# Third tiles paired for a Strassen-Winograd out projection, and attention pieces moved between halves

## The chip, the cores and the metric

The kernel runs on one core of a Trainium2 chip. The metric is the device time in microseconds: the median of several executions. A core has five engines that run side by side, each with its own instruction stream in order: TensorE (PE; matmuls from SBUF into PSUM; PEld in the profile is its load of stationary operands), VectorE (DVE), ScalarE (ACT), GpSimd (POOL) and SyncE (SP, which here only issues transfers). They wait for each other through semaphores. PSUM has eight banks of 512 float32 columns per partition.

## What is computed

A local attention, and on its output a feed-forward block with a relu gate (cut to what matters):

```
# attention: q, k, v of shape (4 batches, 8 heads, 768 positions, 64)
scores = q @ k.T / 8 - slope[head] * distance     # kept: 96 positions back, and 8 global keys
a = softmax(scores);  x = a @ v                    # x: (3072 tokens, 512)
# feed-forward, d_model 512, d_ff 1536
h = relu(x @ w_gate) * (x @ w_val)
out = h @ w_out                                    # (3072, 512)
```

## The kernel before

The 3072 tokens are taken as eight halves (half a batch, 384 tokens each), numbered c = 0 to 7; `s` numbers the same halves in the attention. A half has three tiles of 128 tokens, n = 0, 1, 2.

*The feed-forward block of a half* is built by `ffn_pieces(c)` (L509) as two lists of items with a weight each, f1 and f2. f1 has, for each of the twelve blocks `fc` of 128 hidden columns, a gate (four matmuls of 384 columns with `wg`, then a relu on ScalarE, L525) and a val (four matmuls with `wv`, then a product with the relu on VectorE into `ht`, L531). From half 2 on the first two items are split (`begin`): six of the eight matmuls of fc = 0 first, then the last quarter of the gate and of the val, which need the last part of `xT`.

f2 is the out projection. In half 0 it is plain: for each tile, four items of three matmuls of 512 columns (`outp`, L538), a copy on ScalarE, a store. From half 1 on only the third tile is plain; tiles 0 and 1 are taken together by Strassen's scheme: the four blocks are two tiles by two halves of the hidden columns, and seven products (p1 to p7) of six matmuls with 256 columns each (`block`, L583) replace eight. They use sums of activations (`sum_cb`, `sum_ad`, `sum_de` on VectorE, L567, L571, L576), five sums of weight blocks, computed once in half 1 (`wo_sum`, L809), three ScalarE copies from PSUM and six VectorE passes (L611 to L629) that combine the products into two float32 tiles `osb`. Two products (p6, p7) add onto a bank that holds p3 or p1 already. Some sums are put behind val items (`behind`), the others between the items of f2.

*The attention of a half* is a list of 26 pieces from `attention_pieces(s)` (L493), in four pairs of heads p. `piece_qk(s, p, g)`: g = 0 issues all scores of the pair into four PSUM banks (`pair_scores`, L397) and two exps (L406); g = 1 the other two exps and the masks of the first two banks on VectorE (L359); g = 2 the other masks. `piece_av(s, p, e)`: five (or four) matmuls with the values (L427), a log on ScalarE (L436) and, for e = 1, an exp (L441) that gives the reciprocal of the sums. `piece_norm(s, p)`: two VectorE products (L446) that write `xT`. An empty piece, `gap`, keeps some apart.

*The early pieces* of a half s bring queries and keys: casts on GpSimd (L363), three transposing transfers on SyncE (L368), and GpSimd copies that put the keys in order (L259 to L265). Loads of q and k are issued on SyncE and those of v on GpSimd, at the start of a half's turn.

*The order* is written out by hand. In turn c, `weave` (L664) issues the items of f1 + f2 of half c and, after each, every placed piece whose position (a fraction of the summed weights) has been reached. `spread` (L659) gives evenly spaced positions: in turn c the attention of half c + 1 stands between 0.0 and 0.8 (0.07 and 0.82 for c = 2), the early pieces of half c + 2 between 0.25 and 0.75. Half 0's last third, half 1's last third and their out projections are woven with the attention of half 2, whose last piece, the norm of the last pair, is issued after everything else of that turn. Half 7 has no attention beside it. Each engine takes its instructions in the order in which they were issued.

PSUM from half 1's last third on: three banks "ff" for gates, vals and some products, five banks "x" for attention and the other products, each pool used in rotation. `ht` has two buffers, `osb` three.

Of the kernel before, what the change touches and what calls it, by code (L numbers as in the profile page):

```python
# [8 lines left out]
FP32 = mybir.dt.float32  # L9
BF16 = mybir.dt.bfloat16  # L10
AF = mybir.ActivationFunctionType
ALU = mybir.AluOpType
# [3 lines left out]
def kernel(  # L16
# [12 lines left out]
    nc = tc.nc  # L29
# [4 lines left out]
    DM = H * D  # L34
# [473 lines left out]

    def ffn_pieces(c):  # L509
# [43 lines left out]

        N2, D2 = N_FC // 2, DM // 2
        tiles_ = [slice(n * 128, (n + 1) * 128) for n in range(2)]

        def sums_of(name, *shape):
            if name not in st:
                st[name] = late["sums"].tile([128, *shape], BF16, name=name)
            return st[name]  # L560

        cb = lambda: sums_of("cb", N2, 2, 128)
        ad = lambda: sums_of("ad", N2, 128)
        de = lambda: sums_of("de", N_FC, 128)

        def sum_cb(i0, i1):
            nc.vector.tensor_tensor(cb()[:, i0:i1].rearrange("f i n t -> f i (n t)"), ht[:, i0:i1, 0:256],  # L567
                                    ht[:, N2 + i0 : N2 + i1, 0:256], op=ALU.add)

        def sum_ad(i0, i1):  # L570
            nc.vector.tensor_tensor(ad()[:, i0:i1], ht[:, i0:i1, tiles_[0]],  # L571
                                    ht[:, N2 + i0 : N2 + i1, tiles_[1]], op=ALU.add)

        def sum_de(i0, i1):
            x, y = (1, 0) if i0 < N2 else (0, 1)
            nc.vector.tensor_tensor(de()[:, i0:i1], ht[:, i0:i1, tiles_[x]], ht[:, i0:i1, tiles_[y]],  # L576
                                    op=ALU.subtract)

        def block(key, pool, left, right, start, stop):
            if start:  # L580
                st[key] = psum[pool].tile([128, 512], FP32, name=f"{pool}_ps")
            for i in range(N2):
                nc.tensor.matmul(st[key][:, 0:D2], lhsT=left(i), rhs=right(i),  # L583
                                 start=start and i == 0, stop=stop and i == N2 - 1,
                                 skip_group_check=not start)
            return st[key][:, 0:D2]

        c0, c1 = slice(0, D2), slice(D2, DM)
        bs = lambda name: lambda i: late["bs"][name][:, i]
        V2 = nc.vector.tensor_tensor  # L590

        def store(n, cols, eng=nc.sync):
            eng.dma_start(out=out_v[c, n][:, cols], in_=st["r", n][:, cols])

        def p4():
            for n in range(2):
                st["r", n] = late["osb"].tile([128, DM], FP32, name="osb")
            ps = block("d", "ff", lambda i: ht[:, N2 + i, tiles_[1]], bs("b21-b11"), True, True)
            nc.scalar.copy(st["r", 0][:, c0], ps)

        def p3():
            ps = block("c", "ff", lambda i: ht[:, i, tiles_[0]], bs("b12-b22"), True, True)
            nc.scalar.copy(st["r", 0][:, c1], ps)

        def p1():
            ps = block("a", "ff", lambda i: ad()[:, i], bs("b11+b22"), True, True)
            nc.scalar.copy(st["r", 1][:, c1], ps)

        def p2():
            ps = block("b", "x", lambda i: cb()[:, i, 1], lambda i: wo_sb[:, i, c0], True, True)  # L610
            V2(st["r", 1][:, c0], ps, st["r", 0][:, c0], op=ALU.add)  # L611
            V2(st["r", 1][:, c1], st["r", 1][:, c1], ps, op=ALU.subtract)

        def p5():
            ps = block("e", "x", lambda i: cb()[:, i, 0], lambda i: wo_sb[:, N2 + i, c1], True, True)
            V2(st["r", 0][:, c1], ps, st["r", 0][:, c1], op=ALU.add)
            V2(st["r", 0][:, c0], st["r", 0][:, c0], ps, op=ALU.subtract)
            if c == NHALF - 1:
                store(1, c0)
                store(0, c1)  # L620

        def p6():
            ps = block("c", "ff", lambda i: de()[:, i], bs("b11+b12"), False, True)
            V2(st["r", 1][:, c1], ps, st["r", 1][:, c1], op=ALU.add)
            store(1, slice(0, DM) if c < NHALF - 1 else c1, nc.sync if c < NHALF - 1 else nc.scalar)

        def p7():
            ps = block("a", "ff", lambda i: de()[:, N2 + i], bs("b21+b22"), False, True)
            V2(st["r", 0][:, c0], ps, st["r", 0][:, c0], op=ALU.add)  # L629
            store(0, slice(0, DM) if c < NHALF - 1 else c0)  # L630

        behind = {2: [lambda: sum_de(0, 3)], 5: [lambda: sum_de(3, 6)], 8: [lambda: sum_cb(0, 3)],
                  9: [lambda: sum_ad(0, 3)], 10: [lambda: sum_de(6, 9)]}

        def val_and_sums(fc):
            val(fc)
            for f in behind.get(fc, ()):
                f()

# [7 lines left out]
        if c >= 2:  # L647
            f1[:2] = [(1.0, begin_of[c][0]), (0.15, begin_of[c][1]), (0.15, begin_of[c][2])]
# [230 lines left out]
```

## Time and profile before

| | us |
|---|---|
| median of 3 executions | 241.33 (241.17 to 242.48) |
| the profiled execution | 241.74 |
| its span, first to last instruction | 239.9 |
| mean granted TensorE clock | 0.998 of full speed |

| turn | from, us | what TensorE does |
|---|---|---|
| start, halves 0 and 1 | 0 to 79 | attention 0 and 1, feed-forward 0 and 1, attention 2 |
| half 2 | 79 to 104.8 | feed-forward 2, attention 3 |
| half 3 | 104.8 to 131.4 | feed-forward 3, attention 4 |
| half 4 | 131.4 to 159.2 | feed-forward 4, attention 5 |
| half 5 | 159.2 to 186.2 | feed-forward 5, attention 6 |
| half 6 | 186.2 to 213.8 | feed-forward 6, attention 7 |
| half 7 | 213.8 to 236.6 | feed-forward 7 |

The page gives each engine's busy time, the chain of work that ended last, and groups of instructions by source line. "L583 PE MATMUL ... x84 | 10.3, 272 | 0.0" reads: line 583, 84 matmuls, busy 10.3 us in all, 272 ns for one, no idle time in front of them. Matmuls overlap, so one lasts longer than the distance between two starts; the distance is read from the timeline, whose rows give start, length, engine, line, operation, tiles, shape and count, and in brackets the engine's idle time before and what ended it.

### The profile page before, as it was taken

To read this page: it belongs to the slowest core of one execution; us is meant where nothing else is said; L and a number is where in the kernel's file an instruction comes from. 1 tells how busy PE (TensorE), PEld (TensorE's weight loads), DVE (VectorE), ACT (ScalarE), POOL (GpSimd) and SP (SyncE) were. 2 spreads that over 40 slices of the span, in tenths; PEclk is the share of its full clock that TensorE was granted. 3 is DMA by queue.
4 is the path that set the end of the run, shared out by engine and by line. 5 is a ranking of instruction groups with operands and counts; after the bars stand their busy time and mean duration, and the time that the engine had idled before them with its cause. 6 is when DMAs were issued, how large, how long until landed. Compare 5 with 4: busy or idle time off the path is not lost.

```text
span 239.9 us, 5355 instructions
## 1 busy us (share of the span) xinstructions
PE 233.5 (97%) x1937; PEld 146.6 (61%) x1945; DVE 173.3 (72%) x456; ACT 153.4 (64%) x347; POOL 85.9 (36%) x202
## 2 busy tenths in 40 slices
PE   7899999999999999999999999999999999999994
PEld 3655555665458566666668566676658566676663
DVE  7775955869677788777787687866887677764643
ACT  5897883337775777748774777638774677733330
POOL 6767893208414860903274060902350000000000
PEclk9999999999999999999999999999999999999999
DMA  6999999993976997098519939398431200030003
GB/s 200 181 198 177 257 234 219 185 162 61 270 178 134 301 150 131 8 185 257 108 25 122 285 93 133 19 166 262 67 68 44 90 0 0 3 129 3 4 27 104
DMA packets 69603, 31.42 MB, mean 131 GB/s; under 512 B 47160, under 2 KB 66616, under 8 KB 69576
## 3 DMA queue, kind: packets, MB, share of 16 engines
q0 software_dynamic: 31744, 8.71, 35.3%
q1 hardware_dynamic: 36616, 21.45, 35.1%
q10 hardware_dynamic: 1216, 0.92, 1.2%
q8 instruction: 15, 0.25, 0.4%
q14 instruction: 12, 0.10, 0.1%
HBM read 28.41 MB, written 6.29 MB: 145 GB/s over the span
## 4 chain that ended last, share of the span: by engine, by line
PE 91%; ACT 3%; DVE 2%; issue 1%; ACTq 0%
PE ff_ps L518 53%; PE ff_ps L538 9%; PE ff_ps L583 8%; PE x_ps L427 6%; PE x_ps L397 4%; PE x_ps L583 3%; PE t_ps L459 2%; PE s_ps L341 2%; PE t_ps L272 1%; PE t_ps L682 1%; ACT lnd L436 1%; PE t_ps L310 1%; DVE xT L446 1%; PE s_ps L321 1%; ACT rcp L441 0%
## 5 line engine op out<-in xcount | busy, mean ns | idle before, releaser
L518 PE MATMUL ff_ps<-xT,wg 128*128 128x384 bf16 x384 | 80.7, 326 | 0.5 <-ACT grelu L525 0.4
L518 PE MATMUL ff_ps<-xT,wv 128*128 128x384 bf16 x384 | 80.2, 326 | 0.0
L531 DVE TENSOR_TENSOR ht<-ff_ps,grelu 128x384 bf16<-128x384 f32 x96 | 53.1, 554 | 28.5 <-PE ff_ps L518 13.8
L525 ACT ACTIVATE grelu<-ff_ps 128x384 bf16<-128x384 f32 x96 | 47.1, 492 | 39.4 <-PE ff_ps L518 20.9
L518 PEld LDWEIGHTS <-wg 128*128 128x128 bf16 x384 | 35.9, 98 | 23.9 <-issue 0.9
L518 PEld LDWEIGHTS <-wv 128*128 128x128 bf16 x384 | 36.1, 97 | 23.4 <-issue 1.2
L406 ACT ACTIVATE es<-x_ps 128x360 bf16<-128x360 f32 (+2 forms) x96 | 36.8, 444 | 16.9 <-PE x_ps L397 16.8
L359 DVE TENSOR_TENSOR es<-es,m_all 128x432 bf16<-128x432 bf16 (+4 forms) x108 | 31.2, 334 | 8.2 <-ACT es L406 7.8
L446 DVE TENSOR_TENSOR xT<-x_ps,rcp 64x384 bf16<-64x384 f32 x48 | 26.6, 554 | 9.4 <-ACT rcp L441 8.8
L436 ACT ACTIVATE lnd<-x_ps 64x384 f32<-64x384 f32 x48 | 23.3, 485 | 12.5 <-PE x_ps L427 11.8
L538 PE MATMUL ff_ps<-wo_sb,ht 128*128 128x512 bf16 x112 | 29.6, 379 | 0.4
L363 POOL CAST kqc<-ks 128x384 bf16<-128x384 f32 x24 | 11.6, 532 | 32.3 <-DMA ks<-in_k_dram 32.3
L137 POOL DMA_DIRECT2D vbuf<-in_v_dram x25 | 21.6, 880 | 2.6 <-DMA wv<-in_moe_w_val_dram 2.1
L427 PE MATMUL x_ps<-es,vbuf 128*128 128x216 bf16 (+4 forms) x216 | 21.8, 225 | 0.0
L427 PEld LDWEIGHTS <-vbuf 128*128 128x128 bf16 x216 | 15.8, 97 | 7.7
L538 PEld LDWEIGHTS <-ht 128*128 128x128 bf16 x120 | 10.8, 97 | 9.8 <-issue 0.2
L263 POOL COPY kT<-kqT 128x240 bf16<-128x240 bf16 x16 | 6.9, 430 | 23.0 <-DMA kqT<-kqc 20.5
L363 POOL CAST kqc<-qs 128x384 bf16<-128x384 f32 x24 | 11.6, 522 | 8.1 <-DMA qs<-in_q_dram 8.1
L259 POOL COPY kT<-kqT 128x360 bf16<-128x360 bf16 x10 | 6.0, 604 | 19.9 <-DMA kqT<-kqc 19.9
L441 ACT ACTIVATE rcp<-lnd 128x384 f32<-128x384 f32 x24 | 12.6, 524 | 0.7
L347 ACT ACTIVATE ef<-s_ps 128x720 bf16<-128x720 f32 (+2 forms) x16 | 10.9, 710 | 2.1 <-PE s_ps L341 1.8
L397 PE MATMUL x_ps<-kqT,kT 64*128 64x216 bf16 (+4 forms) x216 | 11.8, 224 | 0.2
(115 smaller groups left out, 252.8 us busy)
## 6 DMA issues: line engine op xcount, KB each, us to landing
out_dram<-osb SPq DMA_DIRECT2D x22, 256.0 KB, 2.7
ks<-in_k_dram SPq DMA_DIRECT2D x6, 768.0 KB, 5.5
qs<-in_q_dram SPq DMA_DIRECT2D x6, 768.0 KB, 12.1
vbuf<-in_v_dram POOLq DMA_DIRECT2D x21, 120.0 KB, 7.9
wg<-in_moe_w_gate_dram POOLq DMA_DIRECT2D x3, 512.0 KB, 7.9
wv<-in_moe_w_val_dram POOLq DMA_DIRECT2D x3, 512.0 KB, 9.8
wo_sb<-in_moe_w_out_dram POOLq DMA_DIRECT2D x1, 1536.0 KB, 19.6
kq<-in_q_dram ACTq DMA_DIRECT2D x2, 192.0 KB, 4.7
```

The source lines that it names most:

```text
L137: nc.gpsimd.dma_start(out=v_dst(b, NG + r0, NG + r0 + n, j), in_=v[b, :, KT * j + r0 : KT * j + r0 + n, :].rearrange("h p d -> p h d"))
L359: nc.vector.tensor_mul(for_all, for_all, mk)
L363: nc.gpsimd.tensor_copy(kqc[:, :, i].rearrange("t n (h d) -> t h n d", d=D)[:, 2 * p : 2 * p + 2], of[s][:, 2 * p : 2 * p + 2, :].rearrang ...
L406: nc.scalar.activation(es[:, e, 0:c], banks[e][:, 0:c], AF.Exp, bias=0.0, scale=scale)
L427: nc.tensor.matmul(av3[:, :, a : a + w], lhsT=vb[:, j, z0 : z0 + 128], rhs=es[:, e, c : c + NN * w].rearrange("k (n p) -> k n p", n=NN), s ...
L436: nc.scalar.activation(ln[o0 : o0 + 64], av[d0 : d0 + 64, 0:QH], AF.Ln, bias=0.0, scale=1.0)
L446: nc.vector.tensor_tensor(xT_of[s][r, p, :], av_of[s, p, e][r, 0:QH], av_of[s, p, "r"][r], op=ALU.mult)
L518: nc.tensor.matmul(st[key][:, 0:QH], lhsT=w_of(w, dc, fc), rhs=xT_of[c][:, dc, :], start=(dc == 0), stop=(dc == N_DC - 1))
L525: nc.scalar.activation(gr, psg[:, 0:QH], AF.Relu, bias=0.0, scale=1.0)
L531: nc.vector.tensor_tensor(ht[:, fc, :], psv[:, 0:QH], st["gr", fc], op=ALU.mult)
L538: nc.tensor.matmul(ps2, lhsT=ht[:, fc, n * 128 : (n + 1) * 128], rhs=wo_sb[:, fc, :], start=(fc == 0), stop=(fc == N_FC - 1))
L583: nc.tensor.matmul(st[key][:, 0:D2], lhsT=left(i), rhs=right(i), start=start and i == 0, stop=stop and i == N2 - 1, skip_group_check=not s ...
```

## The change

A new function `winograd(pair, sums, order)` takes the place of the seven products in `ffn_pieces`. It computes two tiles with Winograd's form: four sums of activations (`add(1)` to `add(4)`, the second from the first, the fourth from the second), four sums of weights (t1 to t4, likewise chained), seven products m1 to m7, four ScalarE copies and four VectorE passes. Banks a and b come from "ff", c and d from "x". Onto a are added m1, m6 and m7, onto b m5 and m3, and between them the bank is copied out (m1, m5, m6). The order of the products is an argument: two other products stand between a copy's source and the bank's next use, in half 7's own pair one.

The third tiles of halves 4 and 5 form a further pair, and those of 6 and 7; they are computed at the start of the out projection of half 5 and of half 7, with sums in buffers of their own. Halves 4 and 6 have no third tile in their f2, and their `ht` is kept for the next half.

The split beginning remains in half 2 alone. `osb` has four buffers. The first three attention pieces of halves 5 and 7 (the scores, exps and masks of the first pair of heads) move into turns 3 and 5, among their products; in turns 4 and 6 the rest stands between 0.05 and 0.7, and the last two pieces at 0.76 and 0.84.

```diff
+    def winograd(pair, sums, order):
+        N2, D2 = N_FC // 2, DM // 2
+        last = pair[0][0] == NHALF - 1 and pair[0][2] == 0
...
+        def add(j, i0=0, i1=N2):
+            lower, upper = slice(i0, i1), (N2 + i0, N2 + i1)
+            x, y, op = {1: lambda: (h(1, i0, i1), h(1, *upper), ALU.add),
+                        2: lambda: (s(1)[:, lower], h(0, i0, i1), ALU.subtract),
+                        3: lambda: (h(0, i0, i1), h(1, i0, i1), ALU.subtract),
+                        4: lambda: (h(0, *upper), s(2)[:, lower], ALU.subtract)}[j]()
+            V2(s(j)[:, lower], x, y, op=op)
...
+        def block(key, left, right, start=True):
+            if key not in st:
+                bank(key, "x")
+            for i in range(N2):
+                nc.tensor.matmul(st[key][:, 0:D2], lhsT=left(i), rhs=right(i),
+                                 start=start and i == 0, stop=i == N2 - 1, skip_group_check=not start)
+            return st[key][:, 0:D2]
...
+        def m1():
+            for key in "ab" if last else "ba":
+                bank(key, "ff")
+            nc.scalar.copy(r(0, 0), block("a", raw(0, 0), of_b(0, c0)))
+
+        def m2():
+            V2(r(0, 0), block("c", raw(0, 1), of_b(1, c0)), r(0, 0), op=ALU.add)
+            if last:
+                store(0, c0, nc.scalar)
+
+        def m3():
+            V2(r(0, 1), block("b", of_s(4), of_b(1, c1), False), r(0, 1), op=ALU.add)
+            store(0, c1 if last else slice(0, DM))
+
+        def m4():
+            nc.scalar.copy(r(1, 0), block("d", raw(1, 1), of_t(4)))
+
+        def m5():
+            nc.scalar.copy(r(1, 1), block("b", of_s(1), of_t(1)))
+
+        def m6():
+            nc.scalar.copy(r(0, 1), block("a", of_s(2), of_t(2), False))
+
+        def m7():
+            ps = block("a", of_s(3), of_t(3), False)
+            V2(r(1, 0), ps, r(1, 0), op=ALU.subtract)
+            V2(r(1, 1), ps, r(1, 1), op=ALU.add)
+            store(1)
...
+    PAIRED = (4, 6)
...
+        plain = range(NN) if c < 1 else () if c - c % 2 in PAIRED else (NN - 1,)
+        add, products = winograd([(c, ht, 0), (c, ht, 1)], "sums", (1, 5, 6, 4, 7, 2, 3) if c == NHALF - 1 else
+                                 (1, 2, 5, 6, 4, 3, 7) if c in PAIRED else (1, 5, 4, 6, 2, 3, 7))
+        behind = {2: [lambda: add(3, 0, 3)], 5: [lambda: add(3, 3, 6)], 8: [lambda: add(1, 0, 3)],
+                  9: [lambda: add(2, 0, 3)], 10: [lambda: add(4, 0, 3)]}
+        rest = tuple(lambda j=j: add(j, 3, 6) for j in (1, 2, 4))
+        if c in PAIRED:
+            third_of[c] = ht
+        elif c - 1 in PAIRED:
+            add3, products3 = winograd([(c, ht, NN - 1), (c - 1, third_of[c - 1], NN - 1)], "sums3",
+                                       (1, 5, 4, 6, 2, 3, 7))
+            behind.update({1: [lambda: add3(1)], 6: [lambda: add3(2)], 7: [lambda: add3(3)]})
+            rest = (lambda: add3(4),) + rest
...
-        if c >= 2:
-            f1[:2] = [(1.0, begin_of[c][0]), (0.15, begin_of[c][1]), (0.15, begin_of[c][2])]
         if c == 2:
-            f1[0] = (1.5, f1[0][1])
+            f1[:2] = [(1.5, begin_of[c][0]), (0.15, begin_of[c][1]), (0.15, begin_of[c][2])]
             f1[3] = (0.15, lambda: gate(1, N_DC - 1))
         if c >= 1:
-            f2 += [(0.65, f) for f in (p4, p3, p1, p2, p5, p6, p7)]
-            for at, f in ((5, lambda: sum_de(9, 12)), (3, lambda: sum_cb(3, 6)), (2, lambda: sum_ad(3, 6))):
+            f2 += (products3 if c - 1 in PAIRED else []) + products
+            places = (2, 3, 5) if plain else (0, 1, 2) if c in PAIRED else (0, 1, 2, 3)
+            for at, f in list(zip(places, rest))[::-1]:
                 f2.insert(at, (0.0, f))
...
+    ahead = {}
     for c in range(2, NHALF):
         placed = []
-        if c + 1 < NHALF:
-            placed.append(spread(attention_pieces(c + 1), *((0.07, 0.82) if c == 2 else (0.0, 0.8))))
         if c + 2 < NHALF:
             load_qk(c + 2, 0, H)
             load_v_half(c + 2)
             placed.append(spread(early_pieces(c + 2), 0.25, 0.75))
+        if c + 1 < NHALF:
+            pieces = ahead.pop(c + 1, None) or attention_pieces(c + 1)
+            if c in PAIRED:
+                placed.append([(0.76, pieces[-2][1]), (0.84, pieces[-1][1])])
+                placed.append(spread(pieces[:-2], 0.05, 0.7))
+            else:
+                placed.append(spread(pieces, *(0.07, 0.82) if c == 2 else (0.0, 0.8)))
+        if c + 1 in PAIRED:
+            ahead[c + 2] = attention_pieces(c + 2)
+            placed.append(spread([ahead[c + 2].pop(0) for _ in range(3)], *(0.885, 0.975) if c - 1 in PAIRED else (0.82, 0.93)))
```

112 lines of the change are left out of this document (38 added, 74 removed).

## The prediction

> **What bounds the kernel.** I read the page's busy shares first, then its chain, then the chain in order of time.
>
> ```profile
> span 239.9 us, 5355 instructions
> PE 233.5 (97%) x1937; PEld 146.6 (61%) x1945; DVE 173.3 (72%) x456; ACT 153.4 (64%) x347; POOL 85.9 (36%) x202
> PE 91%; ACT 3%; DVE 2%; issue 1%; ACTq 0%
> ```
>
> TensorE is busy 97% and carries 91% of the chain; VectorE and ScalarE have a quarter to a third of the span free. A busy TensorE may still be waiting, so I looked at how far apart its matmuls start. The chain in order of time, in the last half (tokens half 7, where no attention runs), has this row:
>
> ```profile
> 213.85 15.60 PE ff_ps L518 x96
> ```
>
> 96 matmuls of 384 columns in 15.60 us are 0.1625 us each, with nothing between them. The same part of the timeline gives the out projection (columns: start, length, engine, line, count; one of the twelve L538 records is missing in the trace):
>
> ```profile
> 229.28 2.75 PE L538 MATMUL ff_ps<-wo_sb,ht 128*128 128x512 bf16 x11
> 231.88 1.47 PE L583 MATMUL ff_ps<-bs,ht 128*128 128x256 bf16 x12
> 232.73 0.37 ACT L599 COPY osb<-ff_ps 128x256 f32<-128x256 f32 x1
> 233.19 0.82 PE L583 MATMUL ff_ps<-bs,ad 128*128 128x256 bf16 x6
> 235.42 0.42 DVE L616 TENSOR_TENSOR osb<-x_ps,osb 128x256 f32<-128x256 f32 x1
> 235.75 0.41 DVE L617 TENSOR_TENSOR osb<-osb,x_ps 128x256 f32<-128x256 f32 x1
> 236.53 0.37 ACTq L593 DMA_DIRECT2D out_dram<-osb  x1
> 236.66 0.42 DVE L629 TENSOR_TENSOR osb<-ff_ps,osb 128x256 f32<-128x256 f32 x1 [0.16 <-PE ff_ps L583]
> ```
>
> Twelve 512-column matmuls take 231.88 - 229.28 = 2.60 us (0.217 each), twelve 256-column ones 233.19 - 231.88 = 1.31 us (0.109 each). A Strassen product of six is 0.655 us. So the kernel is a stream of matmuls at their column rate, and a change is worth the columns that it removes, plus or minus the few places where the stream stops.
>
> **The change, part by part.** (1) *Third tiles of halves 4 to 7.* Before, each is twelve matmuls of 512 columns; after, two pairs of seven products, 84 matmuls of 256 columns. 48 x 0.217 = 10.40 us leave, 84 x 0.109 = 9.17 us come: **-1.23 us**, all of it on the path. The load of the weights does not limit the short ones:
>
> ```profile
> L583 PEld LDWEIGHTS <-cb 128*128 128x128 bf16 x84 | 8.2, 98 | 0.9
> L576 DVE TENSOR_TENSOR de<-ht 128x384 bf16<-128x384 bf16 x28 | 11.0, 392 | 0.6
> L567 DVE TENSOR_TENSOR cb<-ht 128x768 bf16<-128x768 bf16 x14 | 7.8, 554 | 0.2
> L809 DVE TENSOR_TENSOR bs<-wo_sb 128x768 bf16<-128x768 bf16 x10 | 5.5, 553 | 0.1
> ```
>
> 98 ns of load against 109 ns of spacing. A rule of the Trainium skill speaks against this step: "TensorE: Matmul & The Clock Gate", section "Back-to-back issue gap", gives a stream of loads and matmuls in a real kernel about 81 ns each at 128 columns and about 131 ns at 512. Worked out from these figures as an estimate (98 ns at 256, on a straight line), the change would lose 84 x 98 - 48 x 131 ns = 1.9 us instead of winning 1.23. The rows above, 0.217 and 0.109, disagree with it, so it stays a rival with a small chance.
>
> (2) *The nine pairs of products.* Before, a pair has eight sums of activations (four of 392 ns, two of 554, two shorter), three ScalarE copies and six VectorE passes over PSUM; after, eight sums of 384 columns, four copies and four passes. The two added pairs bring four sums of 768 columns (0.55) each. The weight sums fall from ten to eight, of 553 ns. All that lies beside matmuls: VectorE, the fuller of the two, is idle a sixth of the time even in the fullest half (row under (5)), and the chain has 2% of it; without that cover an extra ScalarE copy would cost its 0.37 us per pair. Cost 0.
>
> What is new is that both open banks are written, copied out by ScalarE and then added to: a product that reuses a bank waits for a copy, and every later matmul waits behind it. A copy is 0.37 us (L599) and begins 0.20 us after the next product could (231.88 + 0.655 = 232.53, copy at 232.73), so it is done 0.57 us into the next product; two products between leave 1.31 - 0.57 = 0.74 us to spare, which is one and a half ScalarE operations of half a microsecond. In half 7 one product lies between: 0.655 - 0.57 = 0.08 us to spare, with an idle ScalarE. I take 0, and leave the rest to a rival. The first sums needed (from the last val of a half) come after one or two products that read raw tiles; cost 0 too.
>
> (3) *End of half 1.* Its last VectorE work is the norm of the next attention, emitted after all products; the next gate's last part waits for it:
>
> ```profile
> 77.09 0.42 DVE L629 TENSOR_TENSOR osb<-ff_ps,osb 128x256 f32<-128x256 f32 x1
> 77.44 1.11 DVE L446 TENSOR_TENSOR xT<-x_ps,rcp 64x384 bf16<-64x384 f32 x2
> 77.87 1.06 PE L518 MATMUL ff_ps<-xT,wg 128*128 128x384 bf16 x4
> 78.77 0.32 PE L518 MATMUL ff_ps<-xT,wv 128*128 128x384 bf16 x1
> ```
>
> Before, one VectorE pass (L629) follows the last product, then the norm to 78.55. TensorE should go on at 77.87 + 4 x 0.1625 = 78.52 and does at 78.77: it stands still for 0.25 us. After, the last product (m7) has two passes. They start 0.33 us apart (L616 to L617), so the norm and the matmul behind it come later: **+0.33 us**. Bounds: 0, if VectorE got there earlier, to 0.42, a whole pass.
>
> (4) *The start of halves 3 to 7.* The split beginning goes; the same 768 matmuls remain. Halves 4 and 6 each began with a wait:
>
> ```profile
> 132.95 0.79 ACT L406 ACTIVATE es<-x_ps 128x336 bf16<-128x336 f32 x2 [3.47 <-PE x_ps L397]
> 133.34 0.81 PE L518 MATMUL ff_ps<-xT,wg 128*128 128x384 bf16 x4
> 133.63 0.50 ACT L525 ACTIVATE grelu<-ff_ps 128x384 bf16<-128x384 f32 x1
> 134.18 0.81 PE L518 MATMUL ff_ps<-xT,wv 128*128 128x384 bf16 x4
> ...
> 188.04 0.81 PE L518 MATMUL ff_ps<-xT,wg 128*128 128x384 bf16 x4
> 188.87 0.81 PE L518 MATMUL ff_ps<-xT,wv 128*128 128x384 bf16 x4
> ```
>
> 133.34 + 4 x 0.1625 = 133.99, but the next starts at 134.18: the relu stood behind two exps. The second time 188.69 against 188.87. After, the first scores of these two halves are taken a half earlier and the first relu has ScalarE to itself: **-0.37 us**. Bounds: 0 (another exp takes the place) to -0.37.
>
> (5) *Attention placed anew.* The first scores of attention 5 and 7 move into the products of halves 3 and 5, with four exps and their masks. Their keys must be there:
>
> ```profile
> 121.29 0.42 POOL L263 COPY kT<-kqT 128x240 bf16<-128x240 bf16 x1 [5.90 <-DMA kqT<-kqc]
> 122.00 0.38 POOL L265 COPY kT<-kqT 128x48 bf16<-128x48 bf16 x1
> 126.94 1.47 PE L583 MATMUL ff_ps<-bs,ht 128*128 128x256 bf16 x12
> ...
> 152.90 0.23 POOL L261 COPY kT<-kT 128x56 bf16<-128x56 bf16 x1
> 159.20 0.49 PE L518 MATMUL ff_ps<-xT,wg 128*128 128x384 bf16 x2
> 176.49 0.56 POOL L263 COPY kT<-kqT 128x240 bf16<-128x240 bf16 x1 [6.13 <-DMA kqT<-kqc]
> ```
>
> In half 3 the scores come after two products, 126.94 + 1.31 = 128.3, six us after the first pair's keys (122.38). In half 5, which starts at 159.20, the keys come 17 us later, and the scores after eleven products on top of 24 pieces of 0.65, some 23 us plus attention. GpSimd's casts, and the loads and transposes on SyncE, keep their order. They get the same fraction of a half 4 that is 3.1 us shorter (2.60 of long matmuls and half a microsecond of scores); its last keys came at 153.13, 6.1 us before half 5, so 3.0 us are left. Stores on SyncE: one fewer in each of halves 4 and 6 (none for a third tile), one more in 5; in either kernel SyncE waits for VectorE's last pass before it issues the next loads, which come 0.33 us later. Cover: those 3 to 6 us; beyond them TensorE would wait for GpSimd at the scores. In halves 4 and 6 the remaining pieces stand 0.96 items apart (21 in 0.65 of 31), against 1.08 before and 1.01 in half 2, which has ScalarE and VectorE this full:
>
> ```profile
> 79.00:104.80 25.80, 25.75 (x221) 16.96 (x221) 21.34 (x53) 18.84 (x44) 14.01 (x28) 1.00 0.96 145
> 152.51 0.67 PE L427 MATMUL x_ps<-es,vbuf 128*128 128x216 bf16 x5
> 153.66 0.47 PE L427 MATMUL x_ps<-es,vbuf 128*128 128x216 bf16 x5
> ```
>
> (TensorE, loads, VectorE, ScalarE, GpSimd.) Half 2 runs its TensorE without a stop at 73% and 83%. A late mask costs what it costs in half 4 now: five matmuls in 0.67 instead of 0.47. I allow one such new wait, **+0.20 us**; bounds 0 and, with a half microsecond in each of the two halves, 1.0.
>
> (6) *The tail.* The last pass, store and landing are the same; but a full tile's store goes out two products before the end, where there was half a tile (L593). **+0.1 us**, between 0 and 0.37, one more issue ahead of the last.
>
> Sum: -1.23 + 0.33 - 0.37 + 0.20 + 0.10 = **-0.97 us**. The profiled execution took 241.74 us (1.8 around its span), 0.4 above the median; against the median of 241.33 the forecast is **240.4 us**.
>
> **The rivals.** *More is won* (0.20): the norm at the end of half 1 and the new waits cost nothing: -1.23 - 0.37 = -1.6, 239.7 us. For it: VectorE has fewer passes in all; against: the order of the two last passes is fixed by the code.
> *Nothing is won* (0.10): the tighter attention in halves 4 and 6 stops TensorE for about half a microsecond in each, so that relus hold its banks: 1.0, of which 0.2 is in the sum: 241.2. For it: 83% VectorE; against: half 2.
> *Copies come late* (0.13), the slower side. Where three ScalarE operations of 0.50 us (L525 above) stand in front of a copy, the reuse comes at 3 x 0.50 + 0.57 = 2.07 us instead of 1.31, 0.76 late. At one reuse of five of the nine pairs, those with attention around their products, that is 3.8 us: 244.2 us. It decides from (0.97 + 1.21) / 9 = 0.24 us per pair. For it: the products of half 1 have two lns and an exp among their copies,
>
> ```profile
> 73.83 0.99 ACT L436 ACTIVATE lnd<-x_ps 64x384 f32<-64x384 f32 x2
> 74.86 0.52 ACT L441 ACTIVATE rcp<-lnd 128x384 f32<-128x384 f32 x1
> ```
>
> though there the copies queued behind them still end ahead of the third product; against: elsewhere the attention's pieces are thin among the products, and ScalarE is idle a third of the span. The Trainium skill, "PSUM — Partial Sum Buffer", section "Engine vs sequencer instructions", says that matmuls start and complete in program order; by that rule one late copy is paid in full, as reckoned here, and no row shows a matmul overtaking.
> *Short matmuls pay for their weights* (0.02): with 124 ns each (5.20 us / 42) nothing is saved, and with the whole load of 98 ns on top of 109 the 84 cost 8.2 us more, 248.6. The rows exclude it nearly: the same shapes run at 109 now. The rule weighed under (1) stands beside it.
>
> **How the numbers follow.** The worked sum has 0.55, with its own range 240.0 to 241.0. Half a per cent, 1.21 us, is about what a measurement of this kernel can tell from no change; it ends at 240.12 and 242.54. A fifth of the first case lies below (0.11), with the 0.20 this makes faster 0.31; the rest of it (0.44) and the case of nothing won (0.10) make within 0.54; slower 0.13 + 0.02 = 0.15. The range 239.6 to 242.4 leaves out the two slow cases and the lower edge of the first rival.
>
> **What would show it.** Right: 72 records (less the missing ones) of 512 columns in the out projection, and 378 short ones still 0.109 apart; half 7 about 2.0 us longer and halves 4 and 6 without L538; the wait before the first val of half 2 at about 0.6 us; halves 4 and 6 starting without a late val; the first scores of attention 5 and 7 among products, not held. Wrong: a stop of TensorE before an accumulating product, with ScalarE's copy as releaser; or stops over 0.2 us in halves 4 and 6 behind a mask, a norm or a relu; or scores that wait for GpSimd's keys.

## The result, and the profile after

| | before | after |
|---|---|---|
| median, us | 241.45 (240.99 to 242.56, 22 executions) | 240.73 (240.31 to 241.58, 22 executions) |
| the profiled execution, us | 241.74 | 241.08 |
| its span, us | 239.9 | 239.3 |

The ratio of the times is 0.9971, with a 95% interval of 0.996 to 0.9981: 0.70 us less (0.46 to 0.97), 0.3%. The page of the profile after (busy times, the chain's shares, two groups of the out projection):

```profile
span 239.3 us, 5430 instructions
...
PE 232.4 (97%) x1977; PEld 150.2 (63%) x1981; DVE 172.3 (72%) x456; ACT 156.4 (65%) x358; POOL 86.0 (36%) x202
...
PE 92%; DVE 3%; ACT 2%; DMA 1%; issue 0%
...
L549 PE MATMUL ff_ps<-t,s 128*128 128x256 bf16 x162 | 21.6, 273 | 0.0
...
L627 PE MATMUL ff_ps<-wo_sb,ht 128*128 128x512 bf16 x68 | 17.8, 379 | 0.2
```

TensorE is as busy as before and carries as much of the chain: the kernel is still a stream of matmuls. The long matmuls of the out projection are 68 records (of 72, four are missing in the trace). Their lines have moved: gates and vals are L607 now, the relu L614, the products L549, the copies L566 to L584, VectorE's passes L569 to L589, the sums of activations L535, the product into `ht` L620, the stores L560.

The chain in order of time (start, length, what), at half 7:

```profile
210.97 15.60 PE ff_ps L607 x96
...
229.85 3.27 PE ff_ps L549 x30
```

96 matmuls of 384 columns again take 15.60 us, and 30 of 256 columns take 3.27 us: 0.109 each, as before.

The whole span can be cut at the first gate matmul of each half (the first of the four L518 or L607 matmuls of a half's first item). These places differ by up to 2.1 us from the turns listed ahead of the prediction, which begin half 2 at 79. For each kernel, from one profiled execution, in us, to 0.01; the last column runs from the start of the last matmul to the end of the span, and half 7 ends where that begins:

| | up to half 2 | half 2 | half 3 | half 4 | half 5 | half 6 | half 7 | end |
|---|---|---|---|---|---|---|---|---|
| before | 76.9 | 27.72 | 26.92 | 27.67 | 27.02 | 27.47 | 22.66 | 3.59 |
| after | 76.9 | 28.37 | 27.42 | 24.30 | 29.42 | 24.39 | 24.66 | 3.82 |

Halves 3 to 7 together went from 131.74 to 130.19, half 2 lost 0.65 (0.33 of it at the norm and 0.32 in a stop that e5 and e9 to e12 look into) and the end 0.23. The sum, -0.67, is the difference of the spans (239.94 to 239.29) within 0.02. The timeline of the kernel after at the places of which the prediction spoke (start, length, engine, line, operation, tiles, count; in brackets the idle time before and what ended it):

```profile
77.11 0.42 DVE L588 TENSOR_TENSOR osb<-ff_ps,osb 128x256 f32<-128x256 f32 x1 [0.16 <-PE ff_ps L549]
77.45 0.41 DVE L589 TENSOR_TENSOR osb<-ff_ps,osb 128x256 f32<-128x256 f32 x1
77.78 1.11 DVE L446 TENSOR_TENSOR xT<-x_ps,rcp 64x384 bf16<-64x384 f32 x2
77.92 0.65 PE L607 MATMUL ff_ps<-xT,wg 128*128 128x384 bf16 x3
78.95 0.32 PE L607 MATMUL ff_ps<-xT,wg 128*128 128x384 bf16 x1 [0.38 <-DVE xT L446]
...
129.00 0.48 PE L397 MATMUL x_ps<-kqT,kT 64*128 64x216 bf16 x10
129.41 0.83 PE L549 MATMUL x_ps<-t,ht 128*128 128x256 bf16 x6
131.26 0.39 ACT L584 COPY osb<-ff_ps 128x256 f32<-128x256 f32 x1
132.04 0.82 PE L549 MATMUL ff_ps<-t,s 128*128 128x256 bf16 x6
132.70 0.81 PE L607 MATMUL ff_ps<-xT,wg 128*128 128x384 bf16 x4
133.35 0.81 PE L607 MATMUL ff_ps<-xT,wv 128*128 128x384 bf16 x4
134.00 0.81 PE L607 MATMUL ff_ps<-xT,wg 128*128 128x384 bf16 x4
...
150.38 0.59 PE L427 MATMUL x_ps<-es,vbuf 128*128 128x216 bf16 x5
...
235.65 0.36 ACTq L560 DMA_DIRECT2D out_dram<-osb  x1
235.78 0.42 DVE L574 TENSOR_TENSOR osb<-ff_ps,osb 128x256 f32<-128x256 f32 x1 [0.17 <-PE ff_ps L549]
```

A stop is time by which the starts of two matmuls are further apart than their columns ask for; the step into and out of a group of scores, alike in both kernels, is not counted. A relu or mask is called late where TensorE stops for it, a val where TensorE stops in front of it. Read from the top. At the end of half 1 two passes (L588, L589) stand in front of the norm (L446), and the matmul that needs it starts at 78.95. Three matmuls of 0.1625 from 77.92 on end at 78.41, so TensorE stands still for 0.54 us there, and for 0.04 just before: 0.58 in all, against 0.25 before. In half 3 the moved scores (L397, 129.00) stand among the products; the copy of m6 ends at 131.65, and the matmul that adds onto its bank starts at 132.04, with 0.39 us to spare. Half 4 begins with gate, val, gate 0.65 us apart, without a stop. At 150.38 five matmuls with the values take 0.59 us instead of 0.47, a late mask of 0.12. At the end the last pass (L574) ends at 236.20.

What the table's halves 3 to 7 hold: the late vals of halves 4 and 6 (0.19 and 0.18) and two late masks (0.20 and 0.11) are gone, 0.68; two late masks of 0.12 and one late relu of 0.09 are there instead, 0.34. That makes -0.34, and with the forecast columns (-1.23) -1.57, where -1.55 was measured.

### The profile page after: what moved, and what is told of

Read it like the earlier page. It is cut to its first block, busy times and chain, and to the rows that moved or that the text cites. A ratio compares the mean times of both kernels' runs of the same rounds, so it can differ in the third digit from the quotient of the medians.

```text
span 239.3 us, 5430 instructions
## 1 busy us (share of the span) xinstructions
PE 232.4 (97%) x1977; PEld 150.2 (63%) x1981; DVE 172.3 (72%) x456; ACT 156.4 (65%) x358; POOL 86.0 (36%) x202
## 4 chain that ended last, share of the span: by engine, by line
PE 92%; DVE 3%; ACT 2%; DMA 1%; issue 0%
PE ff_ps L607 52%; PE ff_ps L549 12%; PE x_ps L427 6%; PE ff_ps L627 6%; PE x_ps L549 5%; PE x_ps L397 4%; PE t_ps L459 2%; PE s_ps L341 2%; PE t_ps L272 2%; DMA kq<-in_k_dram 1%; PE t_ps L310 1%; DVE xT L446 1%; ACT lnd L436 1%; PE s_ps L321 1%; ACT ef L347 0%
## 5 line engine op out<-in xcount | busy, mean ns | idle before, releaser
L607 PE MATMUL ff_ps<-xT,wg 128*128 128x384 bf16 x384 | 79.0, 326 | 0.8 <-ACT grelu L614 0.4
L607 PE MATMUL ff_ps<-xT,wv 128*128 128x384 bf16 x384 | 78.6, 326 | 0.0
L614 ACT ACTIVATE grelu<-ff_ps 128x384 bf16<-128x384 f32 x96 | 46.9, 490 | 46.6 <-PE ff_ps L607 24.5
L620 DVE TENSOR_TENSOR ht<-ff_ps,grelu 128x384 bf16<-128x384 f32 x96 | 53.2, 555 | 29.1 <-PE ff_ps L607 18.5
L607 PEld LDWEIGHTS <-wg 128*128 128x128 bf16 x384 | 36.1, 98 | 23.5 <-issue 1.0
L607 PEld LDWEIGHTS <-wv 128*128 128x128 bf16 x384 | 35.7, 98 | 23.9 <-issue 1.2
L406 ACT ACTIVATE es<-x_ps 128x360 bf16<-128x360 f32 (+2 forms) x96 | 35.8, 447 | 3.1 <-PE x_ps L397 3.0
L359 DVE TENSOR_TENSOR es<-es,m_all 128x432 bf16<-128x432 bf16 (+4 forms) x108 | 30.0, 328 | 6.0 <-ACT es L406 5.9
L446 DVE TENSOR_TENSOR xT<-x_ps,rcp 64x384 bf16<-64x384 f32 x48 | 26.6, 554 | 7.5 <-ACT rcp L441 6.8
L549 PEld LDWEIGHTS <-s 128*128 128x128 bf16 x216 | 21.1, 98 | 2.4
L549 PE MATMUL ff_ps<-t,s 128*128 128x256 bf16 x162 | 21.6, 273 | 0.0
L627 PE MATMUL ff_ps<-wo_sb,ht 128*128 128x512 bf16 x68 | 17.8, 379 | 0.2
L549 PEld LDWEIGHTS <-ht 128*128 128x128 bf16 x162 | 15.5, 98 | 2.5 <-DVE xT L446 0.2
L363 POOL CAST kqc<-qs 128x384 bf16<-128x384 f32 x24 | 12.1, 543 | 8.3 <-DMA qs<-in_q_dram 8.3
L535 DVE TENSOR_TENSOR s<-ht 128x384 bf16<-128x384 bf16 (+1 forms) x32 | 13.3, 416 | 0.9
L441 ACT ACTIVATE rcp<-lnd 128x384 f32<-128x384 f32 x24 | 12.6, 524 | 0.8
```

Source lines behind the costliest of these rows:

```text
L359: nc.vector.tensor_mul(for_all, for_all, mk)
L363: nc.gpsimd.tensor_copy(kqc[:, :, i].rearrange("t n (h d) -> t h n d", d=D)[:, 2 * p : 2 * p + 2], of[s][:, 2 * p : 2 * p + 2, :].rearrang ...
L406: nc.scalar.activation(es[:, e, 0:c], banks[e][:, 0:c], AF.Exp, bias=0.0, scale=scale)
L446: nc.vector.tensor_tensor(xT_of[s][r, p, :], av_of[s, p, e][r, 0:QH], av_of[s, p, "r"][r], op=ALU.mult)
L607: nc.tensor.matmul(st[key][:, 0:QH], lhsT=w_of(w, dc, fc), rhs=xT_of[c][:, dc, :], start=(dc == 0), stop=(dc == N_DC - 1))
L614: nc.scalar.activation(gr, psg[:, 0:QH], AF.Relu, bias=0.0, scale=1.0)
```

## The experiments

Times compared with the kernel before are medians and ratios with their 95% interval. None of e1 to e8 leaves out any of the computation. The table of halves again, from one profiled execution of each:

| | up to half 2 | half 2 | half 3 | half 4 | half 5 | half 6 | half 7 | end |
|---|---|---|---|---|---|---|---|---|
| e1 | 76.3 | 28.30 | 26.90 | 27.28 | 26.90 | 27.29 | 22.66 | 4.16 |
| e2 | 76.4 | 27.66 | 27.42 | 24.31 | 29.41 | 24.39 | 24.66 | 3.83 |
| e3 | 78.2 | 28.47 | 27.42 | 24.53 | 29.97 | 24.63 | 24.66 | 3.81 |
| e4 | 77.7 | 28.42 | 26.96 | 25.99 | 28.89 | 25.48 | 24.66 | 3.83 |
| e5 | 76.3 | 27.86 | 27.42 | 24.30 | 29.61 | 24.39 | 24.66 | 3.82 |
| e6 | 76.9 | 28.09 | 27.43 | 27.24 | 27.52 | 26.97 | 22.67 | 3.81 |
| e7 | 76.4 | 28.37 | 27.43 | 24.29 | 29.57 | 24.39 | 24.66 | 3.60 |
| e8 | 76.8 | 27.47 | 27.42 | 24.30 | 29.45 | 24.39 | 24.66 | 3.59 |
| e9 (after again) | 76.8 | 28.05 | 27.43 | 24.30 | 29.91 | 24.40 | 24.66 | 3.82 |
| e10 (before again) | 76.6 | 27.71 | 26.92 | 27.47 | 27.09 | 27.47 | 22.67 | 3.60 |
| e11 (after, third) | 78.4 | 28.25 | 27.43 | 24.30 | 29.41 | 24.39 | 24.66 | 3.82 |
| e12 (before, third) | 77.2 | 28.04 | 26.91 | 27.72 | 27.13 | 27.46 | 22.67 | 3.60 |

The first column moves by up to 1.6 us between executions of one kernel (76.8, 76.9 and 78.4 for the changed one), the later columns by a few tenths. So one execution's span can't settle an edit of half a microsecond, but its halves can.

### e1: third tiles plain, attention as before

```diff
-    PAIRED = (4, 6)
+    PAIRED = ()
```

> The changed kernel with third tiles plain and no attention piece moved between halves; Winograd's products, the shorter split beginning and the norm behind two passes stay. Theory (the columns of the third tiles are the gain): +0.33 at the end of half 1, up to +0.33 for the new wait in half 2, about +0.2 in the tail, -0.37 at the start of halves 4 and 6: 0.2 to 0.9 us slower than the kernel before, 0.9 to 1.6 slower than the changed one. Rival (the gain comes from fewer VectorE passes and the new placement, the third tiles being a wash): as fast as the kernel before or faster, within 0.3 us of the changed one if placement adds nothing.

Measured: 242.0 us, ratio 1.0029 (1.0013 to 1.0045). Everything of the change but the pairs of third tiles and the moved attention is slower than the kernel before by 0.7 us, and slower than the whole change by some 1.4 us. In the columns, half 2 is 0.58 longer than before (0.33 of it the norm, as after) and the end 0.57 (4.16 in this execution, where an 8 KB transfer on q14, an instruction queue by the page, runs from 238.04 to 238.35, behind the last store; e6, with the same end but without such a transfer, has 3.81). Halves 3 to 7 are 0.71 shorter. From half 2 on that makes 0.44 (0.09 with the end of e6) of the 0.70 (0.31 to 1.09); where the rest lies is open. Halves 4 and 6 of this run have no stop at all, though no scores were moved: 27.28 and 27.29 us, against 27.67 and 27.47. So the late vals go without moving scores. Of what this run keeps of the change, the unsplit beginning is what stands at that place; no run changes it alone. The late masks of the kernel before (0.20 and 0.11) are gone here too.

### e6: the placing alone

```diff
-    PAIRED = (4, 6)
+    PAIRED, PLACED = (), (4, 6)
...
-            if c in PAIRED:
+            if c in PLACED:
...
-        if c + 1 in PAIRED:
+        if c + 1 in PLACED:
...
```

> The changed kernel with third tiles plain, but attention placed as in the changed kernel, its first scores moved a half earlier. Theory (the paired third tiles give 1.23 us if the attention's placing is as in the changed kernel): 1.1 to 1.4 us slower than the changed kernel, about as slow as the one with plain third tiles and the old placing. Rival (the placing is worth something by itself, as the loss with the old placing seems to say): clearly faster than that one, by 0.5 us or more.

Measured: 242.31 us, ratio 1.0033 (1.0017 to 1.0049), no better than e1, and by the ratios 1.5 us slower than the whole change (1.1 to 1.4 expected). Its halves 3 to 7 take 131.83 us, 1.64 more than after. Its stops there are two in half 4's mask (0.30 and 0.17), one of 0.10 in half 5, one of 0.09 and one of 0.12 in half 6: 0.78, where after has 0.34. The first two, in the timeline of e6:

```profile
151.40 0.94 PE L427 MATMUL x_ps<-es,vbuf 128*128 128x216 bf16 x5
```

Five matmuls with the values in 0.94 instead of 0.47. 1.64 less (0.78 - 0.34) is 1.20: the price of the columns by itself, forecast as 1.23. This run differs from the changed kernel in the third tiles and, with them, in the order of the products of halves 4 and 6.

### e4: third tiles paired, attention placed as before

```diff
-            if c in PAIRED:
+            if False:
...
-        if c + 1 in PAIRED:
+        if False:
```

> The changed kernel with third tiles paired, but attention placed as before the change (evenly from 0.0 to 0.8 in halves 3 to 6, no piece moved to another half). Theory (third tiles alone carry the gain, placement little): within 0.4 us of the changed kernel and 0.8 to 1.6 us faster than the one without paired third tiles. Rival (halves 4 and 6 have lost 2.6 us of matmuls, so that attention in its old place stops TensorE through full banks): 1 us or more slower than the changed kernel, with waits in halves 4 and 6.

Measured: 242.49 us, ratio 1.0037 (1.0019 to 1.0055): slower than before, and 1.6 us slower than the whole change. My expectation was wrong, and the rival was right in size but not in mechanism. Halves 3 to 7 take 131.98 us, 1.79 more than after, and the stops in them are 0.06 in half 3, 0.22, 0.08, 0.22 and 0.75 in half 4 and 0.74 and 0.03 in half 6: 2.10, against 0.34. The long one of half 4, in the timeline of e4:

```profile
155.00 1.15 PE L549 MATMUL ff_ps<-t,s 128*128 128x256 bf16 x9
155.15 1.13 DVE L446 TENSOR_TENSOR xT<-x_ps,rcp 64x384 bf16<-64x384 f32 x2
156.32 0.36 DVE L535 TENSOR_TENSOR s<-s,ht 128x384 bf16<-128x384 bf16 x1
156.73 0.50 PE L549 MATMUL ff_ps<-t,s 128*128 128x256 bf16 x3 [0.59 <-DVE s L535]
```

The last norm of the attention (L446, 1.13 us) stands on VectorE in front of a sum (L535) that the next product needs. In a half without a third tile no long plain matmuls lie between the last val and the products that read sums, so nothing covers the norm: TensorE waits for the sum until 156.73. The long stop of half 6 is of the same kind (a norm at 209.52, TensorE held until 211.11); the two are 1.49 of the 2.10. With the moved pieces this norm comes after the sums. e1, which differs from this run in its plain third tiles alone, has the same placing and no stop in these halves. The run puts all pieces back, not this norm alone; what the others cost is the remaining 0.61. The gain of the columns is kept only with the new placing, though that is worth nothing alone (e6).

### e3: one product between a copy and the bank's reuse

```diff
-        add, products = winograd([(c, ht, 0), (c, ht, 1)], "sums", (1, 5, 6, 4, 7, 2, 3) if c == NHALF - 1 else
-                                 (1, 2, 5, 6, 4, 3, 7) if c in PAIRED else (1, 5, 4, 6, 2, 3, 7))
+        add, products = winograd([(c, ht, 0), (c, ht, 1)], "sums", (1, 5, 6, 4, 7, 2, 3) if c == NHALF - 1 else
+                                 (1, 5, 6, 4, 7, 2, 3))
...
-                                       (1, 5, 4, 6, 2, 3, 7))
+                                       (1, 5, 6, 4, 7, 2, 3))
```

> The changed kernel with the order 1 5 6 4 7 2 3 for all pairs: one product, not two, between a copied bank and its reuse. Theory (0.74 us to spare with two, 0.08 with one, and less by each ScalarE operation in front of the copy): TensorE waits for copies in the pairs that run beside attention, above all in half 1 (about 0.75), in all 1 to 3 us slower than the changed kernel. Rival (the copies have time whatever the order): within 0.3 us of the changed kernel.

Measured: 243.2 us, ratio 1.0072 (1.0049 to 1.0095), 2.4 us slower than the whole change. TensorE stops 0.77 us in half 1's products, 0.54 in half 2's, 0.23 in half 4's, 0.56 in half 5's and 0.13 in half 6's. The first two, in the timeline of e3:

```profile
74.80 0.82 PE L549 MATMUL x_ps<-t,ht 128*128 128x256 bf16 x6
75.39 0.52 ACT L441 ACTIVATE rcp<-lnd 128x384 f32<-128x384 f32 x1
75.82 0.35 ACT L584 COPY osb<-ff_ps 128x256 f32<-128x256 f32 x1
76.22 0.82 PE L549 MATMUL ff_ps<-t,s 128*128 128x256 bf16 x6 [0.61 <-ACT osb L584]
...
103.38 0.81 PE L549 MATMUL ff_ps<-t,s 128*128 128x256 bf16 x6 [0.38 <-ACT osb L566]
```

The product in between (74.80) ends at 75.46; the copy (L584) stands behind an exp (L441) and ends at 76.17, and the product that adds onto its bank starts then. This is the mechanism of the rival "copies come late". In the changed kernel, with two products between, no product waits for a copy, and in half 7, where one lies between and ScalarE is idle, none does either.

### e2: the norm three products earlier at the end of half 1

```diff
-    weave(f1_0[G[2]] + f1_1[G[2]] + f2_0 + f2_1 + [(0.0, pieces.pop()[1])],
+    weave(f1_0[G[2]] + f1_1[G[2]] + f2_0 + f2_1[:-3] + [(0.0, pieces.pop()[1])] + f2_1[-3:],
```

> The changed kernel with the norm at the end of half 1 issued before its last three products. Theory (the wait of 0.58 us at the start of half 2 is the norm behind VectorE's two last passes): the wait falls to 0.1 or less and the time by 0.5 us, to 240.2 us. Rival (TensorE would wait there anyway, for a bank that VectorE now frees later): the time stays within 0.15 us, the wait moves a few matmuls on.

Measured: 240.16 us, ratio 0.9955 (0.9933 to 0.9976). Its interval overlaps that of the change, so the gain is read from the stop itself. The timeline of e2:

```profile
74.97 1.14 DVE L446 TENSOR_TENSOR xT<-x_ps,rcp 64x384 bf16<-64x384 f32 x2 [1.06 <-ACT rcp L441]
...
76.45 0.49 PE L607 MATMUL ff_ps<-xT,wg 128*128 128x384 bf16 x2
...
76.49 0.41 DVE L574 TENSOR_TENSOR osb<-ff_ps,osb 128x256 f32<-128x256 f32 x1
...
76.95 0.48 PE L607 MATMUL ff_ps<-xT,wv 128*128 128x384 bf16 x2
```

The norm is done at 76.11, before the next half starts. What remains is 0.18 us: the two gate matmuls from 76.45 on end at 76.78, and the val starts at 76.95, when the pass of m3 (L574, to 76.90) has released its bank. 0.58 became 0.18, so 0.40 is to be won, where 0.5 was expected: a second wait, for a bank, had stood behind the first.

### e5: one sum of half 2 two items later

```diff
-        behind = {2: [lambda: add(3, 0, 3)], 5: [lambda: add(3, 3, 6)], 8: [lambda: add(1, 0, 3)],
+        behind = {2: [lambda: add(3, 0, 3)], 7 if c == 2 else 5: [lambda: add(3, 3, 6)], 8: [lambda: add(1, 0, 3)],
```

> The changed kernel with one sum of half 2 (the second part of the third sum) issued behind its eighth val instead of its sixth, so that it no longer stands in front of the first norm. Theory (the new wait of 0.42 us in half 2 is that sum, stretched from 0.36 to 0.68 us where GpSimd casts beside it, and the norm behind it): the wait falls below 0.1 us and the time by 0.1 to 0.35 us, as often as the casts meet the sum. Rival (the norm waits for ScalarE's reciprocal): wait and time stay, within 0.1 us.

Measured: 240.36 us, ratio 0.9952 (0.9932 to 0.9972). Again the ratio's interval overlaps. Half 2 went from 28.37 to 27.86, by 0.51, and is shorter than in any of the changed kernel's own profiles (28.05 to 28.37). In the changed kernel a stop of 0.42 us stood there, and the scores behind it, which no longer start two at a time, took 0.09 more:

```profile
86.40 1.86 POOL L363 CAST kqc<-qs 128x384 bf16<-128x384 f32 x4 [1.03 <-DMA qs<-in_q_dram]
87.75 0.51 POOL L363 CAST kqc<-qs 128x384 bf16<-128x384 f32 x1
87.79 0.68 DVE L535 TENSOR_TENSOR s<-ht 128x384 bf16<-128x384 bf16 x1
88.39 1.13 DVE L446 TENSOR_TENSOR xT<-x_ps,rcp 64x384 bf16<-64x384 f32 x2
88.99 0.32 PE L397 MATMUL x_ps<-kqT,kT 64*128 64x192 bf16 x3 [0.27 <-DVE xT L446]
```

(Timeline of the kernel after; the second line is the last of the four casts by itself.) A sum (L535) runs beside GpSimd's casts and takes 0.68 us; the norm behind it releases a PSUM bank late, and the scores wait for that bank. In the timeline of e5 the norm has no sum in front of it, and all ten scores go at once:

```profile
87.22 1.14 DVE L446 TENSOR_TENSOR xT<-x_ps,rcp 64x384 bf16<-64x384 f32 x2
87.78 0.48 PE L397 MATMUL x_ps<-kqT,kT 64*128 64x216 bf16 x10
```

### e9 to e12: both kernels again, unedited

One profiled execution each, to see whether this stop belongs to the change.

> The changed kernel once more, for a second profile of half 2. Theory (the wait in half 2 belongs to the change, whose later norm shifts the casts onto the sum): the wait of 0.3 to 0.5 us is there again. Rival (it hangs on when the load of q lands, and comes and goes): it may be missing.

> The kernel before once more, for a second profile of half 2. Theory (the wait belongs to the change): no wait over 0.1 us in half 2, the sum 0.36 us long. Rival (it hangs on when the load of q lands): the casts may meet the sum here too, with a wait of 0.3 us or more.

> The changed kernel, a third profile of half 2; as for the second.

> The kernel before, a third profile of half 2; as for the second.

The stop in half 2 was 0.42, 0.10 and 0.30 us in the three profiles of the changed kernel, and 0.10, 0.10 and 0.42 in the three of the kernel before. It stands in both: the theory that it is the change's fell, the rival held. How often is another question. In e1, e3, e4, e6 and e7, whose half 2 is the changed kernel's up to there, it was 0.35, 0.30, 0.47, 0.15 and 0.42: with the changed kernel's own three, six of eight profiles have 0.3 us or more, against one of three before. Whether the change makes it more frequent is open. The third profile of the kernel before (timeline of e12; its sum of activations is L576):

```profile
86.32 1.87 POOL L363 CAST kqc<-qs 128x384 bf16<-128x384 f32 x4 [0.75 <-DMA qs<-in_q_dram]
87.72 0.68 DVE L576 TENSOR_TENSOR de<-ht 128x384 bf16<-128x384 bf16 x1
88.32 1.13 DVE L446 TENSOR_TENSOR xT<-x_ps,rcp 64x384 bf16<-64x384 f32 x2
88.92 0.25 PE L397 MATMUL x_ps<-kqT,kT 64*128 64x192 bf16 x2 [0.26 <-DVE xT L446]
```

It is the same picture, the casts, the sum and the norm to 0.01 us. The second profile of the changed kernel (timeline of e9) shows the same sum unstretched at almost the same place, and a stop that is new, in half 5:

```profile
87.70 0.36 DVE L535 TENSOR_TENSOR s<-ht 128x384 bf16<-128x384 bf16 x1
87.77 0.66 POOL L363 CAST kqc<-qs 128x384 bf16<-128x384 f32 x1
87.98 1.13 DVE L446 TENSOR_TENSOR xT<-x_ps,rcp 64x384 bf16<-64x384 f32 x2
...
167.95 2.34 POOL L363 CAST kqc<-qs 128x384 bf16<-128x384 f32 x4 [0.40 <-DMA qs<-in_q_dram]
168.45 0.87 DVE L535 TENSOR_TENSOR s<-s,ht 128x768 bf16<-128x768 bf16 x1
169.24 1.59 DVE L359 TENSOR_TENSOR es<-es,m_all 128x432 bf16<-128x432 bf16 x4
170.76 0.55 DVE L620 TENSOR_TENSOR ht<-ff_ps,grelu 128x384 bf16<-128x384 f32 x1
171.22 0.54 DVE L535 TENSOR_TENSOR s<-ht 128x768 bf16<-128x768 bf16 x1
171.35 0.81 PE L607 MATMUL ff_ps<-xT,wg 128*128 128x384 bf16 x4 [0.34 <-DVE ht L620]
```

The two pictures of half 2 differ in which of the two instructions starts first. In the kernel after the cast starts at 87.75 and the sum at 87.79; the cast takes 0.51 us and the sum 0.68. In e9 the sum starts at 87.70 and the cast at 87.77; the sum takes 0.36 and the cast 0.66, and it is GpSimd that loses the time. A few hundredths of a microsecond between a cast, which follows the landing of a load, and a sum, which follows a val, decide whether TensorE stops.

In half 5 a 768-column sum of the third pair takes 0.87 us beside the casts (the next one, at 171.22, takes 0.54), the four masks behind it 1.59; the product into `ht` comes late, and a gate waits 0.50 us for the bank that it releases. That sum is the change's own. The same stop was 0.20 us in e5 and 0.16 in e7, and absent in after, e2 and e11, so it too comes and goes; half 5's length (29.41 to 29.91) shows it.

### e7: the last store in two parts

```diff
         def m7():
             ps = block("a", of_s(3), of_t(3), False)
             V2(r(1, 0), ps, r(1, 0), op=ALU.subtract)
+            if last:
+                store(1, c0)
             V2(r(1, 1), ps, r(1, 1), op=ALU.add)
-            store(1)
+            if last:
+                store(1, c1, nc.scalar)
+            else:
+                store(1)
```

> The changed kernel with the last full tile stored in two halves, each as soon as its VectorE pass is done, the second from ScalarE's queue. Theory (the tail grew by 0.2 us since a full tile's store and its neighbours reach the transfer engines together): the time from the last matmul to the end falls by 0.1 to 0.25 us. Rival (the last store's landing is a fixed time): the tail stays, within 0.05 us.

Measured: 241.03 us, ratio 0.9969 (0.9951 to 0.9987): not to be told from the change by the time, but the end went from 3.82 to 3.60 us, which is what it was before. The timeline of e7:

```profile
234.63 1.59 SPq L560 DMA_DIRECT2D out_dram<-osb  x2
...
234.96 0.88 ACTq L560 DMA_DIRECT2D out_dram<-osb  x2
235.43 0.42 DVE L574 TENSOR_TENSOR osb<-ff_ps,osb 128x256 f32<-128x256 f32 x1 [0.17 <-PE ff_ps L549]
```

The last pass is as far from the last matmul as after. From its end to the end of the span lie 238.7 - 235.85 = 2.85 us, against 239.29 - 236.20 = 3.09 after and 239.94 - 237.08 = 2.86 before. So the 0.23 us lie behind the last pass, in how the last store gets out. The run shows that the full tile's store just before it causes them: with that store in two parts they are gone. Its first part also goes out one pass earlier, and its second on ScalarE's queue; which of the three matters is not shown.

### e8: e2, e5 and e7 together

> The changed kernel with the norm before the last three products of half 1, the later sum in half 2 and the split last store. If the three are separate causes they add: 0.5 + 0.25 + 0.15, 0.9 us faster than the changed kernel, 239.8 us. If they share their cover, no more than 0.6.

Its edits are those of the three. Measured: 239.58 us, ratio 0.9915 (0.9903 to 0.9927): 2.05 us faster than before, and its interval does not touch that of the change, from which it is some 1.35 us away (0.9 expected; where the other 0.45 lies is open). By the table it wins 0.90 us in half 2 and 0.23 at the end against the profile after; of these, up to 0.3 hang on what that execution had met in half 2. It beats both kernels.

## Why the prediction was right, point by point

The forecast was -0.97 us, the measurement is -0.70 (0.46 to 0.97): 240.73 lies in the likeliest case's own range, and the result is faster by less than half a per cent, the case that had the largest chance. The terms for the columns and the norm came out by their mechanisms. That the total came so near is in part luck: steps (4) and (5) together won 0.17 more than forecast, and the tail and the stops that come and go took back that and 0.27 more.

(1) *Third tiles, -1.23.* Right. Half 7, where no attention runs, is 2.00 us longer (22.66 to 24.66; 42 short matmuls more and twelve long ones less are 42 x 0.109 - 12 x 0.217 = 1.97, and half 6 loses twelve long ones, 2.60), and what is left of halves 3 to 7 without their waits is 1.20 us (against e6) to 1.21 (against before). The weight load of 98 ns stays hidden: 0.109 us per short matmul. The Trainium skill's rule that stood against this step ("TensorE: Matmul & The Clock Gate", section "Back-to-back issue gap") is not what these runs show: 0.109 us at 256 columns and 0.217 at 512, with a load for each.

(2) *The nine pairs, 0.* Right for the copies: no product waits for one. e3 shows that the two products between them are what keeps it so; one between costs 2.4 us, less than the 3.8 of the rival with the late copies, but the same mechanism. The 0.08 us to spare in half 7 held. Not right for the sums everywhere: those of the third pair in half 5 cost 0 to 0.50 us when they meet casts.

(3) *End of half 1, +0.33.* Right: the wait went from 0.25 to 0.58. e2 shows that it is the norm's place in VectorE's queue.

(4) *Starts of halves 4 and 6, -0.37.* Right in size. The reason given, the scores taken earlier, is not needed: e1 loses these waits with no scores moved.

(5) *Attention placed anew, +0.20.* Mis-sized, and by two errors: the placed pieces cost two late masks of 0.12 and a late relu of 0.09, 0.33 where 0.20 was forecast, but the late masks before (0.20 and 0.11), which the step took to stay, are gone. The net is +0.02, and the stop in half 5 adds 0 to 0.50. The case against new waits was half 2, read as running without a stop; its row of busy shares hides one of 0.10 (its third group of ten scores takes 0.60 us, the others 0.41), which was 0.42 in e12. The reasoning failed too: I priced the new placing against the old one in the kernel before. In the changed kernel the old placing costs 1.6 us (e4), mainly because the third tile that covered the last norm is gone. No score waits for its keys. The step set a cost on the moving, and never asked what the work that left had been hiding.

(6) *The tail, +0.1.* Mis-sized: +0.23 in every profile of the changed kernel (3.82 against 3.59 and 3.60), inside the bounds of 0 to 0.37. e7 takes it away.

Between the measured terms (-1.55 in the profile's halves 3 to 7, +0.33, +0.23: -0.99) and the median's -0.70 lie the stops that come and go. Over three profiles each, halves 3 to 7 take 130.36 us (130.19, 130.70, 130.19) against 131.75 (131.74, 131.62, 131.88): -1.39, which makes -0.83 with the same two terms. With half 2 taken whole, its own stop included (28.22 against 27.82, +0.40), it is -0.76. Both lie inside the interval. How often the stops of halves 2 and 5 occur in executions without a profile is open.

The rivals: the copies were not late; nothing like "nothing is won" happened, since halves 4 and 6 keep 0.1 us stops; "more is won" would have needed the end of half 1 and the tail for nothing, and most of both can indeed be had, by e2 and e7.

## What to carry to other kernels

Before work is taken off the critical engine, ask what waits on the other engines' queues it had been covering: here twelve long matmuls hid a norm in front of a sum, and with the attention left in its old place the whole gain was lost. When an accumulator is copied out between two of its additions, count the copy with everything that may stand in front of it on its engine; one product of 0.655 us between was too few beside attention, two were enough. Cut the span at fixed points of the work and compare stage by stage over several executions: the total's own spread was larger than most of the steps.

## What the runs showed of the hardware that was not expected

A VectorE sum of two SBUF tiles takes 0.36 us for 384 columns, and up to 0.73 us where GpSimd's casts run at the same time; for 768 columns 0.55 became up to 0.88. The Trainium skill, "SBUF — State Buffer", section "Who interferes with whom", says that a VectorE instruction with two inputs in SBUF contends with a GpSimd instruction that reads SBUF. The stretched rows agree. Which of the two is stretched follows from their starts: where these differ by more than 0.01 us, the sum of 384 columns or the cast, whichever started first, keeps its length in every profile of this case (0.36 us, and 0.50 to 0.52), and the other takes longer, the more of the first is still to run. The two rows of half 2 under e5 and e9 are an example of each.

Switching TensorE between full matmuls and the scores with 64 rows costs about 0.10 us going in and 0.09 coming back, in halves 2 to 6 of every profile, the two kernels alike: from the last matmul of 384 columns to the first score lie 0.26 us instead of 0.16.
